# Moving the output projection of the third segment behind the opening of the feed-forward buffers

## The chip, the cores and the metric

The kernel runs on one core of a Trainium2 chip. The core has a matrix engine (TensorE, "PE" in the profile, with its weight loads as "PEld"), a vector engine (VectorE, "DVE"), a scalar engine (ScalarE, "ACT"), a general engine (GpSimd, "POOL") and a queue engine that issues the transfers (SyncE, "SP"). Each engine takes its instructions strictly in the order in which they were written for it, and waits for the others by semaphores. The metric is the device time of one execution in microseconds (us), as the median of several runs.

## The reference

One layer over x of 2048 rows and 512 columns, with 32 heads of 16 columns, four segments of 512 rows, and a feed-forward width of 1792:

```python
mod = (_silu(c) @ w_mod).reshape(c.shape[0], 6, 1, -1)
sa, ca, ga, sb, cb, gb = (mod[:, 0], mod[:, 1], mod[:, 2], mod[:, 3], mod[:, 4], mod[:, 5])
h = _layernorm(x, axis=-1) * (1 + ca) + sa
x = x + ga * _A_ref(h, A_wq, A_wk, A_wv, A_wo, A_beta)
h = _layernorm(x, axis=-1) * (1 + cb) + sb
x = x + gb * _B_ref(h, B_w1, B_b1, B_w2, B_b2)
```

`_A_ref` is softmax attention inside each segment of 512 rows (with the mask of the code), mixed by a gate with a linear memory that is summed over the segments before. Its result is multiplied by `wo`: that is the output projection of this text. `_B_ref` is `relu(x @ w1 + b1)**2 @ w2 + b2`.

## The kernel before

**Numbers.** Matrix products are done three times on operands split into a rounded high part and a low part (high*high, high*low, low*high). ACT writes the high part with a cast; DVE or POOL writes the low part as the difference. Most work around the change is of this kind: one cast and one subtraction for each operand tile.

**Stages.** The first stage (to about 431 us) goes over sixteen units `u`: segment `s = u // 4`, eight heads at a time. For each unit it makes queries and keys (`qk`), values (`vproj`), row maxima (`a_quad`), then scores, exponentials, masks and value products (`b_quad`: scores on TensorE at L1144, exponentials on ACT at L1161, masks on POOL at L1148, value products on TensorE at L1203, transposes back at L1238, normalisation on DVE at L1252 to L1255, the sum with the memory's part at L1261), and the memory (`mem`). In the last segment the heads' results stay on the chip in `X1L`; those of the first three go to DRAM (`o_dram`).

The output projection works on sixteen tiles of 128 rows (`wo_tile(g, pr)`, L1313), four for each segment. A tile loads its heads' results and its rows of x (L1321, L1322), turns them (L1332), splits them into a high part on ACT (L1340) and a low part on DVE (L1342), multiplies by `wo` (held in `WVO`), adds x, takes the statistics for the second normalisation (`ln_stats`, L631, L632) and stores the sum as x1 (L1377). Tiles of segments 0 to 2 (`last` false) multiply in two half-height shapes of 64 rows and 256 columns that TensorE runs in pairs (L1358): 48 products a tile. Tiles of segment 3 (`last` true) use 12 full products of 128 rows and 512 columns (`wo_mm`, L1306 to L1308).

The second normalisation for a segment is `ln2(s, pr)` (L1381): a reciprocal root on POOL (L636, L637), then for each tile the application on DVE (L640), transposes, and an affine step on ACT and DVE (L1398, L1400) into `h2raw`. `h2_ops(s, at)` (L1419) makes the seven operands B11, B12 and so on of a fast product of two-by-two blocks with seven multiplications: differences on POOL (L1438), high parts on ACT (L1446), low parts on DVE (L1448).

The second stage is the feed-forward part. `ffn1(s, p)` multiplies a segment's operands with pair `p` of W1 columns (seven pairs for each segment, seven products each at L1652, sums on DVE at L1664 and L1668, the squared ReLU at L1682 to L1686). `ffn2(s, i, p)` multiplies the result with W2 (L1737) and sums over `p`. W1 is prepared during attention, lies in DRAM and is fetched anew for each segment in halves of 1 MB and 0.75 MB (`fetch_w1`, L1581) into three buffers. W2's seven pairs are multiplied with the gate and combined on POOL (`make_w2`, L817, L818), and split on ACT and DVE (L834, L835); pair 0 is built in `w2a`, pairs 2 to 5 in their buffers, and pairs 1 and 6 go through DRAM (`VIA`).

**Memory.** `open_late` (L1273) takes over the place of the projection weights once the last queries, keys and values are made; it brings `h2raw`, `w2a`, five row tiles `T5`, and a pool `wop` with two tiles `oT` for the projection's split inputs. `open_ffn` (L1535) closes the pool of the attention stage (`ph1`) and `wop`, and opens the feed-forward buffers in their place (W2 tiles, the third W1 buffer, `Tx`, the work space `W2s`). A new tile waits only for the users of the old tiles under it. The tiles of segment 3 split their inputs into the third W1 buffer (two tiles, `FF["ot"]`) and into `FF["ao"]`.

**Order.** The program is a list of nodes, made in the order of the code; each has an engine, what it comes after, and what buffers it takes (`get`) and gives back (`put`). `ORDER` gives for each engine the whole order of its nodes, as node numbers. `N_LATE` and `N_FFN` are nodes without work that run `open_late` and `open_ffn`; `N_FFN` comes after every node made before it except a few. TensorE's row of work near the end of attention is the projection tiles of segments 0 to 2 one after the other, product by product, between the scores and value products of units 13 to 15; behind the last value product come the first feed-forward products of segment 0 and the four tiles of segment 3 between them.

```python
    N_FFN = op("NIL", 0.0, open_ffn, -20.0, after=[n for n in PL.nodes if n.seq not in free_of])
    ...
    for t in range(4):
        wo_tile(4 * NS - 4 + t, z - 2 + 0.3 * t)
```

Of the kernel before, what the change touches and what calls it, by code (L numbers as in the profile page):

```python
# [8 lines left out]
F32 = mybir.dt.float32  # L9
# [8 lines left out]
P = 128  # L18
# [61 lines left out]
1878 496 1879-1880 1971 2128 2333 1974 2334 1978 2140 2335 2122 2336 1986 1882 2338-2339 1981 2340 2131 2341 2143 2259  # L80
1990-1992 1994 2457 1997 2458 2264 2459-2460 2267 2001 2152 2462 2004 2463 2238 2246 2464-2465 2249 2009 2013 2270
2159 2014-2015 2273 498 2166 2162 2276 2252 2169 2243 2362 2178 2599 2174 1968 2179 2280 2182 2255 2180 2404 2185 2189
2017 2616 2192 2602-2605 2367 2370 2607 2197 2608-2610 2373 2201-2203 2633 2283 2376 2619-2620 2290 2621-2622 2205
2286 2624-2627 2383 2636-2638 2379 2639 2391 2298 2293 2641-2644 2397 2667 2650 2302-2304 2306 2653 2313 2654-2656
2309 2670-2671 2658 2672-2673 2388 2659-2661 2394 2675 2735 2316 2676-2678 2321 2738 2486 2739-2741 2494 2684 2400
2743-2746 2407 2491 2752 2325-2327 2414 2687 2422 2497 2688-2690 2755 2500 2756 2692-2694 2417 2695 2757-2758 2507
2521 2410 2760-2763 2430 2329 2433 2849 2701 2426-2427 2503 2437 2440 2518 2428 2845 2769 2837 2841 2449-2450 2445
2704-2707 2512 2531 2709-2711 2538 2772-2773 2712 2774 2515 2775 2534 2451 2777 2541 2778 2524 2779 2546 2780 2453
2718 2786 2550-2552 2721 2554 2722-2723 2561 2724 2789 2564 2790 2726-2727 2791-2792 2728 2557 2729 2794 2569 2795
2528 2796-2797 2573-2575 2996 2577 2997 2999 2874 2896 2907 2998 3001-3002 2885 2877-2879 2910-2911 3017-3018 2912  # L90
3019 2913 2899 3020 2880 3000 2900 2888 2901 2889 3348 2902 3338 2890-2891 3022-3023 3353 3038 3021 3041 3039-3040
# [329 lines left out]
def block_kernel(ctx, tc, x, wq, wk, wv, wo, beta, w1, b1, w2, b2, c, wmod, out):  # L421
# [851 lines left out]
    def open_late():  # L1273
# [562 lines left out]
```

## Time and profile before

| what | us |
|---|---|
| median of 3 runs | 751.4 (751.25, 751.4, 754.45) |
| the profiled execution, its own time | 753.9 |
| its span, first to last instruction | 751.8 |
| TensorE busy in the span | 728.3 |
| DVE, ACT, POOL busy | 631.6, 487.3, 490.3 |
| twelve half-height projection tiles (L1358), TensorE busy | 42.5 |
| mean granted TensorE clock | 0.996 |

The profile is of one execution. The time of an execution holds 2.1 us around the span. "Busy" of TensorE counts overlapping products once; a product's record is longer than its step in a row of equal products, so the length of a row is read from the start of its first product to the start of what follows. "Idle before <-releaser" names the work whose end let the engine go on. The rows themselves stand in the prediction.

### The profile page before, as it was taken

The numbers are of one execution on the slowest core, as the hardware profiler recorded it, in microseconds if no ns is written. First come the engines' busy times: TensorE is split into PE (matmuls) and PEld (weight loads), VectorE is DVE, ScalarE is ACT, GpSimd is POOL, SyncE is SP. The second block draws the span as 40 slices with busy tenths as digits, with TensorE's granted clock in tenths as the row PEclk, the third lists the DMA queues.
The fourth block names the chain that finished last, engine by engine and source line by source line (L and its number), as shares of the span: only waits on it lengthen the run. The fifth ranks groups of instructions, "written<-read, shape, count | busy, mean of one in ns | idle before, by whom it ended". The sixth has DMA issues, their size and how long they took to land.

```text
span 751.8 us, 20671 instructions
## 1 busy us (share of the span) xinstructions
PE 728.3 (97%) x7549; PEld 616.1 (82%) x7549; DVE 631.6 (84%) x1684; ACT 487.3 (65%) x1074; POOL 490.3 (65%) x669
## 2 busy tenths in 40 slices
PE   8999999999999999999999989999999999999996
PEld 7776777666777677776787778999999999999996
DVE  5588888898898989889998989788798888867785
ACT  3669877999879986888668836574335442543342
POOL 5776857789858785664775467857555755555662
PEclk9999999999999999999999999999999999999999
DMA  9887864545643454557893188997776677657710
GB/s 312 249 221 238 246 170 125 161 115 163 199 140 101 111 168 100 142 154 248 259 324 117 49 285 287 327 326 268 251 275 235 224 229 240 231 199 241 277 43 29
DMA packets 84608, 151.84 MB, mean 202 GB/s; under 512 B 10134, under 2 KB 32666, under 8 KB 84508
## 3 DMA queue, kind: packets, MB, share of 16 engines
q1 hardware_dynamic: 84356, 150.40, 63.5%
q8 instruction: 60, 0.98, 0.5%
q14 instruction: 40, 0.33, 0.1%
q10 hardware_dynamic: 152, 0.13, 0.1%
HBM read 94.14 MB, written 29.36 MB: 164 GB/s over the span
## 4 chain that ended last, share of the span: by engine, by line
PE 72%; DVE 10%; DMA 9%; ACT 3%; issue 3%; SPq 2%; POOL 1%; DVEq 0%; ACTq 0%; POOLq 0%
PE bm L1737 16%; PE bh L1652 14%; PE bpv L1203 8%; PE bqk L867 7%; PE bv L937 5%; PE ba L975 5%; PE bpb L1144 5%; DMA ST<-w1d 4%; PE bwop L1358 4%; DVE ba L980 2%; DMA ST<-sg 2%; SPq L916 2%; PE bwarm L570 2%; DMA xt<-in_A_x 1%; ACT pt L1161 1%
## 5 line engine op out<-in xcount | busy, mean ns | idle before, releaser
L980 DVE CUSTOM_DVE_ANT_0 ba<-ba,msk 128x384 f32<-128x384 f32 (+2 forms) x384 | 193.0, 531 | 28.0 <-PE ba L975 21.2
L1161 ACT ACTIVATE pt<-bpb 128x512 f32<-128x512 f32 x320 | 174.2, 617 | 11.7 <-PE bpb L1144 10.3
L1148 POOL TENSOR_SCALAR_AFFINE_SELECT pt<-pt 128x512 f32<-128x512 f32 x128 | 79.5, 641 | 66.8 <-ACT pt L1161 43.5
L867 PE MATMUL bqk<-HT,WQK 64*128 64x512 f32 x720 | 104.6, 397 | 0.3 <-ACT HT L843 0.3
L1737 PE MATMUL bm<-w,ST 128*128 128x256 f32 x660 | 94.0, 283 | 1.0 <-DVE ST L1722 0.5
L1737 PEld LDWEIGHTS bm<-w,ST 128*128 128x128 f32 x660 | 85.2, 191 | 1.5 <-DVE ST L1722 0.7
L1203 PE MATMUL bpv<-pt,VT 128*32 128x512 f32 (+3 forms) x1024 | 82.3, 441 | 0.3 <-ACT lnf L657 0.2
L1144 PE MATMUL bpb<-ST 64*128 64x256 f32 (+2 forms) x512 | 80.7, 345 | 1.8 <-DMA ST<-mt 1.1
L1652 PE MATMUL bh<-ST 128*128 128x256 f32 x564 | 79.8, 283 | 2.1 <-DVE ST L1448 2.0
L867 PEld LDWEIGHTS bqk<-HT,WQK 64*128 64x128 f32 x720 | 70.4, 185 | 9.6 <-ACT VT L943 0.8
L975 PE MATMUL ba<-ST 63*128 63x256 f32 (+2 forms) x512 | 76.1, 340 | 1.8 <-DMA ST<-sg 0.9
L1652 PEld LDWEIGHTS bh<-ST 128*128 128x128 f32 x564 | 72.5, 190 | 3.0 <-DVE ST L1448 2.2
L975 PEld LDWEIGHTS ba<-ST 63*128 63x128 f32 x512 | 51.1, 185 | 20.2 <-DVE mx L980 2.5
L1144 PEld LDWEIGHTS bpb<-ST 64*128 64x128 f32 x512 | 52.2, 185 | 18.5 <-issue 3.9
L1203 PEld LDWEIGHTS bpv<-pt,VT 128*32 128x32 f32 x1024 | 27.6, 109 | 33.8 <-issue 25.0
L980 DVE DVE_READ_ACCUMULATOR2_ANT mx<- 128x1 f32 x384 | 54.3, 141 | 0.1
L937 PE MATMUL bv<-WVO,HT 64*128 64x512 f32 x384 | 54.1, 395 | 0.0
L909 POOL TENSOR_SCALAR e<-e 128x512 f32<-128x512 f32 x24 | 35.7, 1489 | 15.4 <-ACT e L905 15.0
L1358 PE MATMUL bwop<-WVO,oT 64*128 64x256 f32 x576 | 42.5, 280 | 0.2 <-DVE am L1078 0.2
L1358 PEld LDWEIGHTS bwop<-WVO,oT 64*128 64x128 f32 x576 | 39.4, 185 | 1.9 <-DVE am L1078 0.5
L937 PEld LDWEIGHTS bv<-WVO,HT 64*128 64x128 f32 x384 | 37.0, 185 | 4.7
L1008 ACT COPY ac<-ba 128x512 f32<-128x512 f32 x64 | 36.0, 600 | 7.1 <-PE ba L975 6.9
(299 smaller groups left out, 1724.4 us busy)
## 6 DMA issues: line engine op xcount, KB each, us to landing
ST<-sg SPq DMA_DIRECT2D x192, 128.0 KB
ST<-w1d SPq DMA_DIRECT2D x20, 1024.0 KB
ST<-w1d SPq DMA_DIRECT2D x18, 768.0 KB
w1d<-X1L SPq DMA_DIRECT2D x21, 512.0 KB
w<-w1d SPq DMA_DIRECT2D x8, 1024.0 KB
w<-w1d SPq DMA_DIRECT2D x10, 768.0 KB
xt<-in_A_x SPq DMA_DIRECT2D x16, 256.0 KB
wm<-in_w_mod SPq DMA_DIRECT2D x16, 256.0 KB
```

Source lines behind the costliest of these rows:

```text
L867: nc.tensor.matmul(bank(banks[w]), W3(w, k, x, cols.start, cols.stop)[r], HT[r, y, k], start=first and i == 0, stop=last and i == 2)
L937: nc.tensor.matmul(bank(banks[t]), HT[r, x, k, (t2 + t) * P:(t2 + t + 1) * P], WVO[r, k, y], start=first and i == 0, stop=last and i == 2)
L975: nc.tensor.matmul(dst[:, c0:c0 + n], ST[b:b + 63, 0, sl, qt * P:(qt + 1) * P], ST[b:b + 63, 1, sl, :n], start=True, stop=True)
L980: nc.vector.tensor_tensor_reduce(i, i, msk[:, 512 - n:], scale=1.0, scalar=-3e38, op0=ALU.add, op1=ALU.max, accum_out=o)
L1008: cp = [act(512, lambda j=j: nc.scalar.copy(buf("ac", ac)[:, j], bank(keys[j])), pr[0] + 0.01 + 0.001 * j, after=[first], put=[keys[j]]) f ...
L1144: nc.tensor.matmul(dst, ST[b:b + 64, 1, sl, kb * P:(kb + 1) * P], ST[b:b + 64, 0, sl, q0:512], start=True, stop=True)
L1148: nc.gpsimd.affine_select(out=ap, in_=ap, pattern=[[0, ap.shape[1]], [1, P]], compare_op=ALU.is_ge, fill=0.0, base=0, channel_multiplier=-1)
L1161: ns = [op("ACT", 0.49, lambda j=j: nc.scalar.activation(buf("PPP"[n], pt)[:, i + j], bank(keys[j]), AF.Exp, scale=0.25), pr[slot] + 0.01 ...
L1203: nc.tensor.matmul(bank(o)[32 * hq:32 * hq + 32, q0:q0 + src.shape[1]], v[:, a:a + 32], src, start=start, stop=stop, tile_position=(0, 32 ...
L1358: nc.tensor.matmul(bank(bs_[c])[:, :256], TL[ot][r, x, k * P:(k + 1) * P], WVO[r, k, y, 256 * c:256 * c + 256], start=turn == i == q == 0, ...
L1652: nc.tensor.matmul(pb(i), A[:, x, kk], B[:, y, kk], start=kk == j == 0, stop=kk == 1 and j == 2)
L1737: nc.tensor.matmul(q if wide else q[:, c * HALF:(c + 1) * HALF], TL[ao][a >= 3][:, x, a_ * P:(a_ + 1) * P], LT["w2z"][:, b:15:14 - b] if w ...
```

## The change

It does six things.

1. `wo_tile` distinguishes `last = s >= 2` (segments 2 and 3) from `end = s == 3`. The tiles of segment 2 are no longer made before `N_FFN` but behind the tiles of segment 3, and use the 12 full products of the `last` branch. Their loads of heads' results and x, and their stores, move with them.
2. All sixteen tiles split their inputs into two tiles `LT["oT"]` that lie in `w1c`, a tile that `open_late` opens and that later is the third W1 buffer. The pool `wop` and `FF["ot"]` go. The third W1 buffer is given free (`("w1h",)`) when all eight last tiles have multiplied.
3. The tiles of segment 3 no longer wait for `N_FFN`; their loads of x come after `N_LATE`. The four tiles `Tx` are held back from the pool of row tiles until `N_FFN` (`("txh",)`).
4. Six low parts go from DVE to POOL: three of W2 pair 0 (`p == W2R`) and three of segment 0's operands (B11, T1, B21).
5. `ln2` of segments 1 to 3 no longer waits for all four x loads of segment 3, and some planned times change.
6. `ORDER` is written anew for all five engines, from about the third unit of segment 2 to the end. In it POOL's subtractions of W2 pair 0 stand among the masks of units 13 and 14, that of T1 among the masks of unit 15, and those of B11 and B21 directly behind the last mask. TensorE's order begins the feed-forward part with S2\*T2, the last transposes, A22\*T4 and A11\*B11, then tiles 14, 13, 15 and 12 (segment 3) and 8, 9, 11 and 10 (segment 2) between the products of pairs 0 to 3. Which W2 pairs are built in their buffers and which go through DRAM stays as it was (pairs 0 and 2 to 5 in place, 1 and 6 through DRAM).

```diff
-            l = op("DVE", (b - a) * HALF / 960 + 0.07, lambda a=a, b=b, o=o: nc.vector.tensor_tensor(
+            gp = p == W2R
+            l = op("POOL" if gp else "DVE", ((b - a) * HALF / 500 + 0.2) if gp else (b - a) * HALF / 960 + 0.07, lambda a=a, b=b, o=o: (nc.gpsimd if gp else nc.vector).tensor_tensor(
...
-        LT["s"] = ExitStack()
-        LT["op"] = LT["s"].enter_context(tc.tile_pool(name="wop", bufs=1, side="right", reuse_waits="tile"))
+        LT["w1c"] = x1p.tile([P, 2, 4, 2, P], F32R, name="w1c")
+        LT["oT"] = [LT["w1c"].rearrange("p h a k n -> p (h a k n)")[:, i * 2 * L:(i + 1) * 2 * L].rearrange("p (h n) -> p h n", h=2) for i in (0, 1)]
...
-        last = s == NS - 1
+        last, end = s >= WL, s == NS - 1
...
-        ld = sp(load, pr - 0.2, 1 << (18 if last else 19), 1 if last else 2, after=heads + [N_FFN if last else N_LATE],
-                get=[("xr", xk)] if last else [("xr", o), ("xr", xk)])
+        ld = sp(load, pr - 0.2, 1 << (18 if end else 19), 1 if end else 2, after=[N_LATE] if end else heads + [N_LATE],
+                get=[("xr", xk)] if end else [("xr", o), ("xr", xk)])
...
-                       after=[n] if k else [h, l, *WON], get=() if k else [("#D", b2)], put=[ot if g % 2 else ("w1h",)] if k == KD - 1 else ())
+                       after=[n] if k else [h, l, *WON], get=() if k else [("#D", b2)], put=[ot, ("w1h",)] if k == KD - 1 else ())
...
-        r = op("POOL", 1.33, lambda: ln_rstd(st_all[:, 4 * s:4 * s + 4]), pr[0] - 0.1, after=[X1N[4 * s + t] for t in range(4)] + (XWN if s else []))
+        r = op("POOL", 1.33, lambda: ln_rstd(st_all[:, 4 * s:4 * s + 4]), pr[0] - 0.1, after=[X1N[4 * s + t] for t in range(4)])
...
+            gp = s == 0 and j in (0, 3, 6)
+            l = op("POOL" if gp else "DVE", 1.24 if gp else 0.6, lambda j=j, name=name: (nc.gpsimd if gp else nc.vector).tensor_tensor(
...
+    PL.held["txh",] = [("T", i) for i in range(5, 9)]
+    for i in range(9):
...
-    for s in range(NS - 1):
+    WL = 2
+    for s in range(WL):
         for t in range(4):
             wo_tile(4 * s + t, e + K_P[s] + 0.3 * t)
...
-        LT["s"].close()
...
-                    for i in (0, 1)] + [sb2.tile([P, 2, 4, 2, P], F32R, name="w1")]
+                    for i in (0, 1)] + [LT["w1c"]]
...
+    for t in range(4):
+        wo_tile(4 * NS - 8 + t, us(3 + 3.5 * t))
...
-        make_w2(p, 2 + 7 * i, (("W2s", 4 * (i % 2)), ("W2s", 2)), ("W2s", 6), [N_FFN, *(WOL if p == W2C else ()), *W2Q.get(p - 2 if i > 1 else None, ())], [n_gb2],
+        make_w2(p, 6 + 7 * i, (("W2s", 4 * (i % 2)), ("W2s", 2)), ("W2s", 6), [N_FFN, *(WOL if p == W2C else ()), *W2Q.get(p - 2 if i > 1 else None, ())], [n_gb2],
...
-            ln2(s, [us(T0 - 34 + 5 * t) for t in range(4)])
+            ln2(s, [us(T0 - 26 + 3.5 * t) for t in range(4)])
```

More of the change, by code (lines that the diff above doesn't have):

```diff
@@ L199 @@
+4257 4321 4261-4262 4265 4331 4240 4333 4343 4345 4242 4354-4355 4357 4371 4373 4356 4360 4358-4359 4362 4361 4383
+4363 4385 4259 4395 4258 4397 4260 4407 4409 4419 4421 4431 4433 4443 4445 4455 4457 4454 4460-4461 4456 4463
+4458-4459 4462
 """,
@@ L1314, in wo_tile @@
         s = g // 4
-        last = s == NS - 1
+        last, end = s >= WL, s == NS - 1
         o, xk, b, b2, ot = ("ot", g), ("xw", g), ("wot", g), ("wop", g), ("oT", g)
-        pool = "ao" if last else "oT"
         def load():
-            if not last:
+            if not end:
                 nc.sync.dma_start(buf("xr", o), o_dram[g * P:(g + 1) * P, :])
@@ L1330, in tr @@
             for k in range(KD):
-                src = X1L[:, g % 4] if last else TL[o]
+                src = X1L[:, g % 4] if end else TL[o]
                 nc.tensor.transpose(bank(b)[:, k * P:(k + 1) * P], src[:, k * P:(k + 1) * P], ident)
-        n = pe("F", 0.355, tr, pr, after=heads + [N_FFN] if last else [ld], get=[("#D", b)] if last and g % 2 == 0 else [("#D", b), (pool, ot)], put=[("on3", g % 4)] if last else [o])
+        n = pe("F", 0.355, tr, pr, after=heads if end else [ld], get=[("#D", b), ("oT", ot)], put=[("on3", g % 4)] if end else [o])
         def hi():
-            if last:
-                TL[ot] = FF["ao"][PL.slot[ot]][1] if g % 2 else FF["ot"][g % 4 // 2]
-            else:
-                TL[ot] = LT["op"].tile([P, 2, D], F32R, name="oT", tag=f"oT{PL.slot[ot]}")
+            TL[ot] = LT["oT"][PL.slot[ot]]
             nc.scalar.copy(TL[ot][:, 0], bank(b))
@@ L1447, in halves @@
                     after=[*([node[name]] if name in node else RAW[s]), *wait], put=put)
-            l = op("DVE", 0.6, lambda j=j, name=name: nc.vector.tensor_tensor(operand(j)[:, 1], blk[name](), operand(j)[:, 0].bitcast(F32),
-                                                                            op=ALU.subtract), at[1 + j] + 0.05, after=[h], put=put, lock=True)
+            gp = s == 0 and j in (0, 3, 6)
+            l = op("POOL" if gp else "DVE", 1.24 if gp else 0.6, lambda j=j, name=name: (nc.gpsimd if gp else nc.vector).tensor_tensor(
+                operand(j)[:, 1], blk[name](), operand(j)[:, 0].bitcast(F32), op=ALU.subtract), at[1 + j] + 0.05, after=[h], put=put, lock=True)
             OPN[s][name] = [h, l]
@@ L1469, in block_kernel @@
     PL.held["w2t",] = [("T", i) for i in range(5)]
-    for i in range(5):
+    PL.held["txh",] = [("T", i) for i in range(5, 9)]
+    for i in range(9):
         PL.pools["T"].remove(i)
@@ L1561, in block_kernel @@
     free_of = {n.seq for n in h2_ops(0, [us(-7 + 0.7 * j) for j in range(8)]) + W2S}
-    N_FFN = op("NIL", 0.0, open_ffn, -20.0, after=[n for n in PL.nodes if n.seq not in free_of])
+    N_FFN = op("NIL", 0.0, open_ffn, -20.0, after=[n for n in PL.nodes if n.seq not in free_of], put=[("txh",)])
     HOME["xr"] = "T"
```

195 lines of the change are left out of this document (96 added, 99 removed), and 13 rows, old and new, of the table ORDER.

## The prediction

> **What bounds the kernel now.** I read the page first, then the stretches ("windows"), then the timeline of TensorE with its waits. Page, engine shares and chain:
>
> ```profile
> PE 728.3 (97%) x7549; PEld 616.1 (82%) x7549; DVE 631.6 (84%) x1684; ACT 487.3 (65%) x1074; POOL 490.3 (65%) x669
> PE 72%; DVE 10%; DMA 9%; ACT 3%; issue 3%; SPq 2%; POOL 1%; DVEq 0%; ACTq 0%; POOLq 0%
> ```
>
> TensorE is busy for 728.3 of 751.8 us. The most that any reordering can win is the remaining 23.5 us. By stretch (columns: PE, PEld, DVE, ACT, POOL busy us; granted clock; DMA share; GB/s):
>
> ```profile
> 0.00:100.00 100.00, 94.97 (x1010) 74.82 (x1011) 74.53 (x218) 71.59 (x163) 72.57 (x95) 1.00 0.84 253
> 350.00:431.00 81.00, 80.77 (x1143) 65.08 (x1135) 74.53 (x218) 60.52 (x133) 50.29 (x65) 1.00 0.59 195
> 431.00:451.00 20.00, 16.48 (x119) 14.34 (x120) 17.29 (x34) 7.47 (x14) 11.44 (x10) 1.00 0.87 285
> 451.00:485.00 34.00, 32.27 (x243) 30.33 (x242) 29.40 (x58) 18.40 (x37) 26.42 (x33) 1.00 0.87 298
> 485.00:732.00 247.00, 243.17 (x2013) 240.80 (x2012) 202.39 (x405) 110.28 (x217) 147.15 (x233) 1.00 0.70 237
> 732.00:751.80 19.80, 13.26 (x111) 13.05 (x109) 11.48 (x19) 5.31 (x10) 6.46 (x9) 0.94 0.08 28
> 344.00:348.00 4.00, 4.00 (x57) 1.69 (x53) 3.43 (x9) 2.69 (x6) 1.44 (x2) 0.66 0.44 118
> ```
>
> Of the 23.5 us, 5.0 lie in the first 100 and 6.5 in the last 20, where this change does nothing or little. From 350 to 431 us the last attention units run with the twelve output-projection tiles of segments 0 to 2 between them, and TensorE has 0.2 us idle. It loses 3.52 us at the border (431 to 451), 1.73 us from 451 to 485, and 3.8 us in the whole feed-forward stretch behind. DVE is at 74.5 of 81 us in the attention stretch, so it is next. The last row shows a granted clock of 0.66 over 4 us; the third that is missing is worth some 1.4 us. The waits at the border and just after (start, duration, operation, idle before and what ended it):
>
> ```profile
> 435.36 1.20 PE L1332 MATMUL bwot<-ident,X1L 128*128 128x128 f32 x9 [0.93 <-DVE X1L L1261]
> 440.07 0.86 PE L1652 MATMUL bh<-ST 128*128 128x256 f32 x5 [1.96 <-DVE ST L1448]
> 445.50 1.66 PE L1652 MATMUL bh<-H2o,ST 128*128 128x256 f32 x12 [0.63 <-DMA ST<-w1d]
> 460.25 0.97 PE L1652 MATMUL bh<-H2o,ST 128*128 128x256 f32 x6 [0.52 <-DMA ST<-w1d]
> 474.50 0.95 PE L1652 MATMUL bh<-ST,w 128*128 128x256 f32 x6 [0.58 <-DMA w<-w1d]
> 483.19 0.94 PE L1652 MATMUL bh<-H2o,ST 128*128 128x256 f32 x6 [0.63 <-DMA ST<-w1d]
> ```
>
> These six, 5.25 us, are what this change can address.
>
> **The change part by part.**
>
> (1) Four tiles (segment 2) leave the attention stretch and come back behind the border, in another shape: 48 half-height products of 256 columns in pairs before, 12 full products of 512 columns after.
>
> ```profile
> 417.16 1.10 PE L1332 MATMUL bwot<-ident,ot 128*128 128x128 f32 x8
> 418.18 2.36 PE L1203 MATMUL bpv<-pt,VT 128*32 128x512 f32 x32
> ...
> 423.17 2.29 PE L1358 MATMUL bwop<-WVO,oT 64*128 64x256 f32 x36
> 425.28 0.40 PE L1144 MATMUL bpb<-ST 64*128 64x512 f32 x2
> ...
> 441.44 0.40 PE L1307 MATMUL bwop<-WVO,w 128*128 128x512 f32 x1
> 444.47 0.40 PE L1308 MATMUL bwop<-WVO,ST 128*128 128x512 f32 x1
> ```
>
> Old shape: 36 from 423.17 to 425.28, 0.0586 us each, so 48 take 2.81 us. New shape: the second to the fifteenth of a row start 441.44 and 444.47, 13 steps of 0.233 us, so 12 take 2.80 us. The transposes are the same on both sides (two tiles 417.16 to 418.18 with the change of shape, about 0.4 us each). Removed: 4 x 3.2 = 12.8 us; added: 4 x 3.2 us. The work of TensorE is **conserved, 0.0 us**. Attention should end some 12 us earlier, near 419 us, and the feed-forward part grows by as much.
>
> (2) Changes of shape. The written TensorE order changes between full, half-height and quarter-width products 142 times before and 147 times after; all five more lie in the attention stretch, where fewer projection products stand between score and value products.
>
> ```profile
> 427.73 0.95 PE L1358 MATMUL bwop<-WVO,oT 64*128 64x256 f32 x11
> 428.61 2.36 PE L1203 MATMUL bpv<-pt,VT 128*32 128x512 f32 x32
> 430.90 0.97 PE L1652 MATMUL bh<-H2o,ST 128*128 128x256 f32 x6
> ```
>
> Eleven products from 427.73 at 0.0586 us end their stream at 428.37; the next shape starts at 428.61: 0.24 us. I take 0.2 x 5 = **+1.0 us** (0 if all fall into waits, 1.2 at most). The Trainium skill, TensorEngine Tiling (Array Packing), Key Properties, says that a change of tiling mode drains TensorE; it gives no price. By that rule each of the five costs, which the gap above agrees with; without it the sum would be 1.0 us lower.
>
> (3) The border. The other engines in the old tail:
>
> ```profile
> 425.58 1.58 ACT L1161 ACTIVATE pt<-bpb 128x512 f32<-128x512 f32 x3
> 431.04 0.59 ACT L1227 COPY oraw<-bpv 128x512 f32<-128x512 f32 x1 [1.52 <-PE bpv L1203]
> 425.46 0.68 DVE L1448 TENSOR_TENSOR ST<-tt,ST 128x512 fp32r<-128x512 f32 x1
> 438.87 1.15 DVE L1448 TENSOR_TENSOR ST<-h2raw,ST 128x512 fp32r<-128x512 f32 x1
> 437.43 3.74 POOL L818 TENSOR_TENSOR W2s<-W2s 128x512 f32<-128x512 f32 x2 [7.16 <-PE bh L1652]
> 421.29 1.30 POOL L1438 TENSOR_TENSOR tt<-tt,h2raw 128x512 f32<-128x512 f32 x1 [1.59 <-DVE H2o L1448]
> ```
>
> The 1.96 us wait goes: that low part (B21, the 1.15 us row) ran beside POOL's W2 work and stood in DVE's queue behind a W2 part (L835); the new order has both on POOL and asks for B21 seventeen groups after the last value product. What is late next? Let E be the end of the last value product. ACT starts its copy about 0.25 us after E (the next product starts at 430.90 after a change of shape, so E is near 430.8; the copy starts at 431.04), and in the new ACT order two casts stand behind it, B22 and then B11, at about 0.5 us pitch: B11's high part is there at E+1.9. Its low part is now on POOL, 1.3 us instead of 0.68: with two handoffs of about 0.25 it reaches TensorE at E+3.7. Before product A11*B11 TensorE has only S2*T2 (0.71), the last transposes (0.5) and A22*T4 (0.71) with their shape changes, 2.5 us: it waits 1.2 us. The X1L sum (L1261) then comes at about the time that this product ends. Next, the first segment-3 tile needs its high part (ACT behind two other casts) and its low part on DVE: another 0.8 us. The last exponentials (0.52 us each by the first row, ten behind the last scores) and the two masks on POOL behind them hold the last value products for 0.1 to 0.9 us; I count 0.4. Sum 2.4 against 3.52: **-1.1 us** (bounds: none of it saved, and all 3.52 saved).
>
> (4) The first W1 loads. With eight tiles instead of four between the products of the first pairs, TensorE asks for W1 more slowly; but the third W1 buffer is the new home of all projection inputs, and it comes free only after the last of the eight. I counted in the order, from the last use of a buffer to the next need: 8.8, 7.1, 8.5, 11.6, 7.8 and 7.0 us of TensorE work. How long a load takes with the queue full:
>
> ```profile
> 452.35 0.53 SPq L1581 DMA_DIRECT2D ST<-w1d  x1
> ```
>
> The load issued at 452.35 is the one that the product at 460.25 waited for: about 7.9 us with others before it (298 GB/s in that stretch; 1 MB alone would be 3.5 us at that rate). So the spans of 7.0 to 8.8 us are about enough, no more. SP's queue gets eight more loads and four stores here, the loads in order behind the first W2 load: if that waits for memory, the W1 load of the second pair waits behind it. In return the four projection stores that held SP for 13.29 us (below) are fewer. As to bytes: 3 MB, 10 us at 298 GB/s, come with 12.8 us more of TensorE work. I take half of the 1.73 us of waits from 451 to 485 as saved: **-0.9 us** (bounds -1.7 and, if loads come late in the same measure, +1.7).
>
> (5) DVE and ACT.
>
> ```profile
> L1342 DVE TENSOR_TENSOR oT<-bwot,oT 128x512 fp32r<-128x512 f32 x12 | 8.1, 685 | 0.7 <-ACT oT L1340 0.6
> 426.06 0.76 DVE L1370 TENSOR_TENSOR xw<-bwop,xw 128x256 f32<-128x256 f32 x2
> 427.33 0.69 DVE L631 BATCH_NORM_STATS2 bs<-xw 128x6 f32<-128x512 f32 x1
> 428.05 0.18 DVE L632 BATCH_NORM_AGGREGATE st_all<-bs 128x2 f32<-128x6 f32 x1
> ```
>
> Per tile DVE has 0.69 + 0.76 + 0.69 + 0.18 = 2.3 us, 9.3 us in four (ACT, at 60.5 of 81 us, loses one cast a tile). They return behind the border, where DVE has room (202 of 247 us). The subtractions that go to POOL take some 2 us more off DVE before E. That leaves DVE about (74.5 - 9.3 - 2) of 69 us, 92% as before: hidden by TensorE's own work as before, **0**. With that cover gone (4) and (3) would carry it: each us that DVE is late at the border is a us of the end.
>
> (6) The end.
>
> ```profile
> 744.39 0.52 PE L1737 MATMUL bm<-WVO,ST 128*128 128x256 f32 x3
> 744.75 0.51 PE L1737 MATMUL bm<-w,ao 128*128 128x256 f32 x3
> 748.27 0.41 DVE L1771 TENSOR_TENSOR Tx<-Tx,bm 128x256 f32<-128x256 f32 x1
> ```
>
> These two short groups, 0.36 us apart, are the last of TensorE, and ten DVE sums in a row end the kernel 3 us behind them. In the new order the first of the two stands before the groups that the sums start with, so the sums start 0.36 us later against TensorE's end: **+0.35 us**, on the path.
>
> (7) Everything else in the feed-forward order is reshuffled; its 3.8 us of idle I take as unchanged (0, bounds -1.9 and +1.9).
>
> Sum: 0.0 + 1.0 - 1.1 - 0.9 + 0.35 = **-0.65 us** against the profiled execution, which took 753.9 us by its own time (span 751.8 and 2.1 around it). That execution lies 2.5 us above the median of the three runs (751.4); I take the difference off the median: **750.7 us**. A measurement of this kernel can tell about 0.5% (3.8 us) from no change.
>
> **The rivals.**
>
> *Faster: the idle time really goes.* For it: eight independent tiles are cover that the old order lacked at just the place where the W1 loads were late; the SP queue waited long for projection stores (below) and is freed earlier. Then the 1.73 us goes, half of the 3.8, the border falls to 1.5 us (-2.0), and the low clock at 344 us does not return (-1.4): 1.35 - 1.7 - 1.9 - 2.0 - 1.4 = -5.7, **745.7 us**. Against it: at the place of the low clock the new order is nearly the old one, and DVE is as full.
>
> ```profile
> 418.08 13.29 SPq L1377 DMA_DIRECT2D x_dram<-xw  x4
> ```
>
> *Slower: POOL's queue holds the masks.*
>
> ```profile
> L1148 POOL TENSOR_SCALAR_AFFINE_SELECT pt<-pt 128x512 f32<-128x512 f32 x28 | 17.7, 646 | 23.1 <-ACT pt L1161 16.9 <-PE bpv L1203 2.1 <-issue 2.1
> ```
>
> POOL gets six subtractions, five of 512 columns at 1.3 us and one of 768, by its length 1.9 us: 8.4 us; before the last value products alone it rises from 50.3 of 81 us (62%) to about 56 of 69 (81%). Four stand in POOL's queue directly among the masks that the value products need, and the pair at 437.43 took 3.74 us, not 2.6, beside a DVE subtraction (438.87). If half of the 8.4 us reaches TensorE, the price is 4.2 us with nothing won: **755.6 us**. It decides once a subtraction stands ahead of a mask whose exponentials are done by more than it lasts. Against it: between 350 and 431 us POOL waited 16.9 us for exponentials before its masks (the row); a queue that waits so much has room. By the Trainium skill, SBUF — State Buffer, Who interferes with whom, a DVE operation with two SBUF inputs and a POOL operation that reads SBUF block each other in full; the 1.15 us row agrees. By that rule the shift makes each such block twice as long, not shorter, which would add up to 6 x 0.6 = 3.6 us.
>
> *The change doesn't do what it says.* The buffers of the feed-forward part lie where attention's own tiles lay, so opening them earlier in the order may start no load earlier: then (4) is 0, and the time is 751.6 us, no change either.
>
> **How the numbers follow.** Forecast with the third rival (both within 0.5%): 0.50. Faster by over 0.5% (below 747.6): 0.31. Slower by over 0.5% (above 755.2): 0.19. The likeliest case itself runs from 748.0 to 754.0; the range reaches into both rivals, with the bounds of (3), (4) and (7) added: 745.6 to 755.8.
>
> **What would show it.** Right: the last value product ends near 419 us; the six waits fall to about 3 us together, one of about 1 us before the product with H2o (L1652) waiting for POOL; no waits for masks above 1 us. Wrong: TensorE idle before value products (L1203) with POOL as the releaser (slower rival), or feed-forward idle from 470 us on under 2 us (faster rival). Three things make the prediction wrong: a clock below 1.0 at the border, a DMA wait of several us behind SP's new loads, or a total idle that moves by more than 4 us in the reshuffled part.

## The result, and the profile after

| what | before | after |
|---|---|---|
| median, 9 runs each on one chip (us) | 754.45 (751.25 to 757.16) | 748.59 (744.37 to 750.32) |
| ratio, 95% interval | 1 | 0.9916 (0.9888 to 0.9945) |
| profiled execution, its own time | 753.9 | 746.45 |
| its span | 751.8 | 744.7 |
| TensorE busy | 728.3 | 724.5 |

The change makes the kernel faster by 0.84%, 6.3 us of 754.45 (4.1 to 8.4 by the interval). The forecast was 0.65 us less, too little to be told from no change, so that its sign came out says little. The gain is that of the rival "the idle time really goes" (-5.7). That the median of 748.59 lies in the stated range, and even in the 748.0 to 754.0 of the likeliest case, is in part luck: the range was counted from 751.4, the median of three runs of the kernel before, and nine runs of it have 754.45. The line of engine shares on the page of the kernel after:

```profile
PE 724.5 (97%) x7405; PEld 612.3 (82%) x7405; DVE 623.7 (84%) x1674; ACT 485.7 (65%) x1070; POOL 495.5 (67%) x675
```

The share of TensorE is 97%, as before. To see where the 7.1 us of span went, cut both executions at 322 us (until about there TensorE's order is the same), at the first feed-forward product, and at the end of TensorE's last product. Stretches of the kernel before (span, busy us of PE, PEld, DVE, ACT, POOL; granted clock; DMA share; GB/s):

```profile
322.00:430.90 108.90, 107.93 (x1426) 82.29 (x1422) 98.86 (x293) 84.14 (x185) 63.80 (x82) 0.98 0.60 192
430.90:745.20 314.30, 305.22 (x2484) 298.62 (x2480) 257.44 (x508) 141.46 (x277) 191.48 (x282) 1.00 0.70 237
```

The same of the kernel after:

```profile
322.00:419.40 97.40, 93.65 (x1215) 67.83 (x1212) 88.40 (x273) 79.12 (x174) 69.71 (x86) 1.00 0.62 196
419.40:738.40 319.00, 316.07 (x2548) 308.01 (x2544) 258.98 (x519) 144.54 (x284) 191.22 (x284) 1.00 0.71 239
```

Attention ends 11.5 us earlier (108.9 to 97.4). The feed-forward part grows by 4.7 (314.3 to 319.0), though TensorE is busy 10.85 us longer in it: its idle time there falls from 9.08 to 2.93 us. In attention the idle time grows, from 0.97 to 3.75. TensorE's waits in the kernel after (start, duration, operation, idle before and what ended it), and the last value product with the first feed-forward product behind it:

```profile
345.98 0.22 PE L1041 MATMUL bat<-ident,mx 64*16 64x64 f32 x1 [1.37 <-DVE tm L1121]
347.75 0.56 PE L976 MATMUL ba<-ST 63*128 63x256 f32 x4 [1.26 <-DVE on L1256]
352.57 1.17 PE L1069 MATMUL bmr<-MB,phi 64*128 64x68 f32 x16 [1.07 <-ACT ac L1009]
...
416.65 2.79 PE L1204 MATMUL bpv<-pt,VT 128*32 128x256 f32 x40
419.38 0.97 PE L1652 MATMUL bh<-H2o,ST 128*128 128x256 f32 x6
...
422.55 0.86 PE L1652 MATMUL bh<-H2o,ST 128*128 128x256 f32 x5 [0.53 <-POOL H2o L1446]
...
456.18 0.50 PE L1309 MATMUL bwop<-WVO,w1c 128*128 128x512 f32 x1 [0.24 <-DVE w1c L1339]
...
492.80 1.67 PE L1652 MATMUL bh<-ST 128*128 128x256 f32 x12 [1.14 <-DMA ST<-w1d]
```

The six waits of before, 5.25 us from 435 to 483, have become one of 0.53 us and one of 0.24 before 485, and one of 1.14 at 492.80. The first has the place and the releaser that the prediction named for A11\*B11 (the low part of B11 on POOL), and half the length. The three in front are new.

### The profile page after: what moved, and what is told of

Same layout as the page of the kernel before. It is cut to its first block, busy times and chain, and to the rows that moved or that the text cites. A ratio compares the mean times of both kernels' runs of the same rounds, so it can differ in the third digit from the quotient of the medians.

```text
span 744.7 us, 20355 instructions
## 1 busy us (share of the span) xinstructions
PE 724.5 (97%) x7405; PEld 612.3 (82%) x7405; DVE 623.7 (84%) x1674; ACT 485.7 (65%) x1070; POOL 495.5 (67%) x675
## 5 line engine op out<-in xcount | busy, mean ns | idle before, releaser
L981 DVE CUSTOM_DVE_ANT_0 ba<-ba,msk 128x384 f32<-128x384 f32 (+2 forms) x384 | 192.9, 531 | 26.9 <-PE ba L976 19.8
L1652 PE MATMUL bh<-ST 128*128 128x256 f32 x600 | 84.4, 283 | 1.1 <-DMA ST<-w1d 1.1
L1652 PEld LDWEIGHTS bh<-ST 128*128 128x128 f32 x600 | 77.1, 190 | 2.0 <-ACT H2o L1443 1.3
L779 POOL TENSOR_TENSOR X1L<-X1L 128x512 fp32r<-128x512 f32 (+1 forms) x28 | 32.2, 1149 | 12.4 <-ACT X1L L778 12.0
L1020 DVE TENSOR_REDUCE mx<-ac 128x4 f32<-128x1024 f32 x32 | 38.9, 1215 | 0.3 <-POOL ac L1017 0.2
```

What stands on the lines that cost most here:

```text
L981: nc.vector.tensor_tensor_reduce(i, i, msk[:, 512 - n:], scale=1.0, scalar=-3e38, op0=ALU.add, op1=ALU.max, accum_out=o)
L1020: reds.append(op("DVE", 1.13, lambda: nc.vector.tensor_reduce(buf("mx", mx).rearrange("p (a t) -> p a t", t=4)[:, :, 1], acv(), axis=AX.X, ...
L1652: nc.tensor.matmul(pb(i), A[:, x, kk], B[:, y, kk], start=kk == j == 0, stop=kk == 1 and j == 2)
```

## The experiments

Names that begin with b_ are variants of the kernel before, those with a_ of the changed kernel; what each leaves out or moves is told below. Each ratio is to the kernel before on the same chip. For all fourteen profiles, three places can be compared: a mark that every kernel has near 140 us (the value products that wait for the logarithm, 140.94 in the kernel before and 140.91 after), the first feed-forward product (E), and the end of TensorE's last product (745.26 before, 738.45 after). The mark takes out what the first 140 us differ by from execution to execution, up to 3.2 us. The places come from one profiled execution of each kernel, the ratios from 6 to 12 runs.

| kernel | E | mark to E | E to TensorE's end | ratio to before, 95% interval |
|---|---|---|---|---|
| before | 430.90 | 290.0 | 314.4 | 1 |
| b_pool6 | 434.83 | 293.9 | 316.8 | 1.0017 (0.9986 to 1.0047) |
| b_less | 430.76 | 290.5 | 315.0 | 0.9999 (0.9970 to 1.0027) |
| b_dve | 431.31 | 289.1 | 312.7 | 0.9996 (0.9971 to 1.0020) |
| b_both | 427.73 | 287.6 | 313.8 | 0.9971 (0.9948 to 0.9994) |
| b_none | 432.89 | 293.2 | 312.2 | 0.9979 (0.9951 to 1.0006) |
| after | 419.38 | 278.5 | 319.1 | 0.9916 (0.9888 to 0.9945) |
| a_dve6 | 419.90 | 279.4 | 319.8 | 0.9922 (0.9896 to 0.9948) |
| a_less | 420.14 | 280.0 | 319.3 | 0.9930 (0.9900 to 0.9960) |
| a_both | 422.15 | 280.5 | 318.4 | 0.9911 (0.9877 to 0.9946) |
| a_less_w1half | 421.69 | 280.3 | 318.6 | 0.9916 (0.9887 to 0.9945) |
| a_none | 421.51 | 280.3 | 319.9 | 0.9896 (0.9848 to 0.9944) |
| a_oldtail | 421.57 | 280.1 | 320.7 | 0.9955 (0.9929 to 0.9981) |
| a_fix | 418.52 | 279.5 | 321.6 | 0.9947 (0.9922 to 0.9973) |

The table is the main finding. Two groups appear: every kernel with the old order takes 288 to 294 us from the mark to E, and 312 to 317 behind it; every kernel with the new order takes 278 to 281 and 318 to 322. What work of the moved tiles is left out hardly matters in either group.

**The six low parts.** The changed kernel with them back on DVE (the diff), and the kernel before with them on POOL (the same two lines the other way round); in `ORDER` their six numbers move between the lists of the two engines:

```diff
-            gp = p == W2R
+            gp = False
...
-            gp = s == 0 and j in (0, 3, 6)
+            gp = False
```

> The changed kernel with its six low parts (three of W2 pair 0, and B11, T1, B21 of segment 0) back on DVE, each as late in DVE's order as its reader allows; everything else as changed. Theory A (cover: the eight independent projection tiles stand between the first feed-forward products, so that operands and W1 halves come in time, wherever the low parts are made): the time stays within 1.5 us of the changed kernel, 0.990 to 0.994 of the kernel before, and TensorE's idle time behind the last value product stays under 4.5 us (2.9 in the changed kernel). Rival B (POOL: the border is better because six low parts left DVE): 3 to 5 us slower than the changed kernel, 0.996 to 0.999, with a wait of 1.5 to 2 us for a low part of DVE back at the border.

> The kernel before with the same six low parts on POOL, placed behind the masks that are due; nothing else of the change. Theory A (cover): no gain, 0.997 to 1.004 of the kernel before; the wait of 1.96 us for B21's low part may go, but the other waits from the border to 485 us stay (over 3 us together). Rival B (POOL): 2 to 3.5 us faster, 0.995 to 0.997, with the border's 3.52 us of idle under 1.5.

Theory A held both times. On DVE the changed kernel has 0.9922 against 0.9916, and the border's waits stay about 1 us:

```profile
422.01 0.86 PE L1652 MATMUL bh<-ST 128*128 128x256 f32 x5 [0.18 <-DVE ST L1446]
423.45 0.85 PE L1652 MATMUL bh<-H2o,ST 128*128 128x256 f32 x5 [0.47 <-DVE H2o L1446]
425.02 0.77 PE L1332 MATMUL bwot<-ident,X1L 128*128 128x128 f32 x5 [0.39 <-DVE X1L L1262]
```

So in the changed kernel the wait of 1.96 us for B21 goes without POOL too, since B21 is asked for later there. In the kernel before, the same shift alone gains nothing that can be measured. Its profiled execution is 757.8 us long against 751.8: attention took 3.9 us more from the mark, and a W1 load was late by 4 us:

```profile
450.52 2.90 PE L1654 MATMUL bh<-H2o,ST 128*128 128x256 f32 x12 [4.11 <-DMA ST<-w1d]
```

So the 1.96 us wait did go in it, and others took its place (7.3 us of waits from E to 490 us).

**Less TensorE work, in the new place and in the old.** In a_less a tile of segment 2 makes 3 of its 12 products, in b_less 12 of its 48:

```diff
-                n = pe("F", 0.699, lambda k=k: wo_mm(bank(b2), TL[ot], k), ...
+                n = pe("F", 0.699, lambda k=k: wo_mm(bank(b2), TL[ot], k) if s > 2 else wo_one(bank(b2), TL[ot]) if k == 0 else None, ...
```
```diff
             def mm(turn, k, i):
+                if s == 2 and i != (KD - 1 if turn else 0):
+                    return
```

> The changed kernel with 9 of the 12 products of each tile of segment 2 left out (the tile's transposes, splits, sum, loads and stores stay): 36 products of 0.233 us, 8.4 us of TensorE work between the first feed-forward products. Theory A (cover: these products hide the W1 loads): W1 waits come back, 1.5 to 3.5 us of them between the last value product and 480 us, and the time falls by 5 to 7 us only (0.982 to 0.985 of the kernel before). Rival (the loads are in time because they are issued earlier, not because of the cover): it falls by the full 8.4 us (0.980).

> The kernel before with the same share left out: 36 of the 48 half-height products of each tile of segment 2, 144 products of 0.0586 us, 8.4 us of TensorE work in the attention stretch. If TensorE bounds that stretch (0.2 us idle in 81), the last value product comes 7 to 8.4 us earlier and the time falls by as much (0.989 to 0.991). If DVE is as near to the bound as its 74.5 of 81 us say, TensorE begins to wait for DVE there: 3 to 6 us (0.992 to 0.996), and what the move won in attention is less than the 12.8 us of the work.

Both fell short of every number that stood there: 0.9930 (the changed kernel has 0.9916) and 0.9999. In the new place all 8.4 us are given back. Waits of a_less:

```profile
455.12 0.48 PE L1312 MATMUL bwop<-WVO,w1c 128*128 128x512 f32 x1 [3.08 <-DVE uuT L1669]
456.81 0.79 PE L1314 MATMUL bwop<-WVO,w1c 128*128 128x512 f32 x1 [0.98 <-DVE w1c L1344]
466.09 2.58 PE L1657 MATMUL bh<-ST 128*128 128x256 f32 x12 [2.11 <-DMA ST<-w1d]
```

These are 6.17 us, and the granted clock from 439 to 475 us is 0.91 (the row stands further below). In the old place the work leaves a stretch that the profile had shown as full, and E stays where it was. The row of b_less for it:

```profile
322.00:430.80 108.80, 104.47 (x1274) 74.75 (x1270) 99.43 (x290) 83.09 (x184) 64.62 (x82) 0.98 0.59 191
```

144 products of 0.0586 us are gone, 8.4 us, but "busy" fell only from 107.93 to 104.47, 3.5 us, and 3.4 us appear as idle time. The other 5 us still count as busy. The likely reason, which was not tried by itself, is the length of the records: a half-height product that stands alone has a record of 0.28 us (the products at 353.69 and 355.61 in the kernel before) against its step of 0.0586, so short waits between products vanish under the records.

**DVE's part, alone and together with TensorE's.** b_dve leaves out most of DVE's sum and statistics for the four tiles; b_both and a_both have both cuts.

```diff
-            n = [dve(256, lambda c=c: nc.vector.tensor_tensor(TL[xk][:, 256 * c:256 * c + 256], ...
+            n = [dve(256, lambda c=c, n_=8 if s == 2 else 256: nc.vector.tensor_tensor(TL[xk][:, 256 * c:256 * c + n_], ...
...
-        X1N[g] = op("DVE", 0.8, lambda: ln_stats(TL[xk], st_all[:, g]), ...
+        X1N[g] = op("DVE", 0.8, lambda: nc.vector.memset(st_all[:, g], 1.0) if s == 2 else ln_stats(TL[xk], st_all[:, g]), ...
```

> The kernel before with part of DVE's work on the four tiles of segment 2 left out: the two statistics instructions of a tile become one small write, and the sums with x shrink from 256 to 8 columns; by the rows 0.87 and some 0.6 us a tile, 5.5 to 6 us of DVE work in four, at the place in the attention stretch where the same tiles' TensorE work was cut without effect. TensorE's work is whole. If DVE alone sets the pace of that stretch, the last value product (430.8 in the kernel before) comes 4 to 5.5 us earlier and the time falls by as much (0.993 to 0.995). If both engines are at their limit there, or the pace is set by ACT or by the loop between them, it falls by under 1.5 us (0.998 to 1.000).

> The kernel before with both cuts: 8.4 us of TensorE work (36 of 48 products a tile) and 5.5 to 6 us of DVE work of the tiles of segment 2. If DVE and TensorE are both at their limit in the attention stretch, so that neither cut alone does anything: the last value product 4.5 to 6 us earlier, time 0.991 to 0.994. If DVE alone sets the pace: the same as with the cut on DVE alone, within 1 us. If neither does (ACT's exponentials): under 1.5 us.

> The changed kernel with the same two cuts on the tiles of segment 2, which now stand between the first feed-forward products (TensorE's cut alone brought 0 there: waits of 3.1 and 1.0 us for DVE and of 2.1 us for a W1 load came in its place). If DVE, 92% busy from 439 to 475 us, is the limit: 3 to 6 us faster than the changed kernel (0.983 to 0.988 of the kernel before). If the loads are the limit (309 GB/s in that stretch): within 1.5 us of the changed kernel, with the W1 waits longer than 2.1 us.

DVE alone brings nothing (0.9996). Both cuts, some 14 us of work on two engines, bring 2.2 us (0.9971), and 2.4 us from the mark to E: well under the 4.5 to 6 us named for two engines at their limit, and above the 1.5 us named for neither. In the new place both bring nothing beyond the changed kernel (0.9911); its waits from 455 to 468 us are 2.65 and 0.98 us for DVE and 2.25 us for a W1 load, nearly those of a_less. So DVE, 92% busy as it is, isn't the bound by itself either.

**The loads.** The changed kernel with TensorE's cut and half of segment 0's W1 bytes:

```diff
-        n = sp(lambda: nc.sync.dma_start(FF_w1(key)[:, :, :n_].bitcast(F32), w1_dram[p][:, :, a:a + n_]), ...
+        n = sp(lambda: nc.sync.dma_start(FF_w1(key)[:, :1 if s == 0 else 2, :n_].bitcast(F32), w1_dram[p][:, :1 if s == 0 else 2, a:a + n_]), ...
```

> The changed kernel with TensorE's cut (36 products of segment 2's tiles) and with only the high parts of W1 fetched for segment 0, which halves the 12.25 MB of these fetches; the products read what lies in the low places. If the loads are the limit where TensorE's cut alone brought nothing: 4 to 8 us faster than the changed kernel (0.980 to 0.986 of the kernel before), and the W1 wait near 466 us is gone. If DVE is the limit: under 2.5 us faster, with the waits for DVE near 455 us as they were (3.1 and 1.0 us).

The W1 wait at 466 is gone and the time is the same (0.9916). The waits for DVE stay and others come:

```profile
457.43 0.76 PE L1312 MATMUL bwop<-WVO,w1c 128*128 128x512 f32 x1 [3.83 <-DVE uuT L1669]
459.12 0.79 PE L1314 MATMUL bwop<-WVO,w1c 128*128 128x512 f32 x1 [0.50 <-DVE w1c L1344]
476.98 0.66 PE L644 MATMUL blnq<-ident,X1L 128*128 128x128 f32 x4 [1.56 <-DVE X1L L640]
```

There DVE has 34.56 us of 36 busy (439 to 475), without the tiles' sums being cut. So neither the cut on DVE (a_both) nor that on the loads brings the time down: it seems that loads and DVE's results stand close behind each other, and between them the tiles' products are free. A kernel relieved of both was not made, so this stays an argument.

**No engine work of the four tiles at all.**

```diff
-            for k in range(KD):
+            for k in range(KD if s != 2 else 0):
...
-        h = act(512, hi, pr + 0.01, after=[n], put=[b])
-        l = dve(512, lambda: nc.vector.tensor_tensor(TL[ot][:, 1], ...
+        h = act(512, hi if s != 2 else lambda: None, pr + 0.01, after=[n], put=[b])
+        l = dve(512, lambda: None if s == 2 else nc.vector.tensor_tensor(TL[ot][:, 1], ...
```

(and the products, the sums and the statistics likewise)

> The kernel before without any engine work of segment 2's four projection tiles (transposes, casts, differences, products and sums left out, the statistics one small write; loads and stores stay). Cutting 8.4 us of TensorE work there brought nothing, cutting DVE too brought about 2 us. If the attention stretch is held by TensorE, DVE and ACT in turn, so that only the whole of a tile's work counts: the last value product comes 10 to 12.5 us earlier than 430.8 and the time falls by 8 to 12 us (0.984 to 0.989). If the pace there is set by something that the tiles have no part in: under 5 us (above 0.993), and the changed kernel's 11.6 us must come from its new order.

> The changed kernel without any engine work of the same four tiles. If they stand in time in which TensorE would otherwise wait for operands and loads: within 2 us of the changed kernel (0.988 to 0.992 of the kernel before), with 8 us or more of waits behind the last value product. If they cost there what the two profiles differ by behind the last value product: 4 to 5 us faster than the changed kernel. If TensorE's work is conserved, as the prediction had it: 11 to 12.8 us faster (0.975).

In the new place the four tiles cost nothing that can be measured (0.9896 without them, 0.9916 with them, each inside the other's interval). The 11 to 12.8 us of conserved work (0.975) are excluded. The 4 to 5 us of the second number are not excluded by a_none's wide interval (0.9848 to 0.9944) alone; against them stand its length from E (319.9 us, 319.1 in the changed kernel) and the three kernels with part of the tiles' work left out (0.9911 to 0.9930). The stretch from 439 to 475 us of the changed kernel, of a_less and of a_none:

```profile
439.00:475.00 36.00, 35.76 (x244) 32.39 (x242) 33.04 (x63) 20.27 (x38) 21.02 (x27) 1.00 0.89 314
```
```profile
439.00:475.00 36.00, 29.83 (x201) 27.60 (x200) 33.65 (x64) 18.97 (x35) 19.64 (x26) 0.91 0.89 309
```
```profile
439.00:475.00 36.00, 26.97 (x171) 24.99 (x171) 28.10 (x55) 16.86 (x32) 19.17 (x28) 0.86 0.91 318
```

TensorE is idle for 0.24, 6.17 and 9.03 us in it. With 14% of a busy 26.97 us lost to the clock, an estimate of 3.8 us, a_none loses 12.8 us here: as much as the four tiles' TensorE work, which the prediction had put at 4 x 3.2. The waits that fill it:

```profile
447.77 1.65 PE L1652 MATMUL bh<-H2o,ST 128*128 128x256 f32 x12 [1.36 <-DMA ST<-w1d]
456.37 2.55 PE L1652 MATMUL bh<-ST 128*128 128x256 f32 x12 [4.04 <-DVE uuT L1668]
460.19 2.90 PE L1652 MATMUL bh<-H2o,ST 128*128 128x256 f32 x12 [1.27 <-DVE h2raw L1397]
467.28 2.93 PE L1652 MATMUL bh<-ST 128*128 128x256 f32 x12 [2.36 <-DMA ST<-w1d]
```

In the old place they cost nearly nothing either: 0.9979, and E is no earlier. The row of b_none:

```profile
322.00:432.90 110.90, 103.73 (x1209) 72.79 (x1205) 94.48 (x279) 79.86 (x175) 65.00 (x82) 0.95 0.61 197
```

The granted clock is 0.95 in it against 0.98 before, which on 103.73 busy us is some 3 us more lost; without that E would stand about where it does in the kernel before, still no earlier. So the tiles' work going away is not enough: with the old order it can go, and attention lasts as long. How much the order does shows where most of the gain arises. Six groups of 32 value products into the stretch (the sixth starts at 387.67 us before, at 385.73 after), the changed kernel is 2 us ahead; the other 9.5 us come in the last four groups. These last groups in the kernel before, in b_none and in the kernel after:

```profile
390.10:430.90 40.80, 40.80 (x587) 32.84 (x585) 37.19 (x107) 34.41 (x75) 18.66 (x26) 1.00 0.29 100
```
```profile
392.50:432.90 40.40, 38.16 (x433) 25.54 (x433) 31.38 (x94) 32.63 (x70) 19.07 (x26) 0.96 0.36 126
```
```profile
388.10:419.40 31.30, 31.30 (x435) 22.77 (x431) 27.78 (x87) 28.86 (x65) 21.61 (x27) 1.00 0.51 168
```

With nearly the same products (433 and 435), the old order takes 40.4 us and the new one 31.3. Taking 154 products out of the old order wins 0.4 there. The new order is thus needed for the gain. Whether it would win as much with the tiles still in attention isn't shown: in the changed kernel the trace has no gap of TensorE left in these 31.3 us. And "the new order" means here all that b_none keeps as before: it still has the four tiles' loads, stores and buffers in the old place, and no run moves these alone.

**What in the order.** At the end of attention in b_none ACT stands out. Some of its instructions there (start, duration, operation):

```profile
421.39 0.62 ACT L1446 CAST H2o<-tt 128x512 fp32r<-128x512 f32 x1
...
426.10 3.03 ACT L1161 ACTIVATE pt<-bpb 128x512 f32<-128x512 f32 x6
428.97 0.66 ACT L1446 CAST ST<-h2raw 128x512 fp32r<-128x512 f32 x1
429.48 0.88 ACT L834 CAST w2a<-T 128x768 fp32r<-128x768 f32 x1
430.21 1.14 ACT L1161 ACTIVATE pt<-bpb 128x512 f32<-128x512 f32 x2
```

Casts of the feed-forward part stand in ACT's queue in front of the last exponentials, and ACT has few gaps. The kernel before is alike: of the 16 us from 414 to 430 ACT is busy for 15.22.

```profile
414.00:430.00 16.00, 16.00 (x242) 12.91 (x238) 14.49 (x41) 15.22 (x32) 7.25 (x10) 1.00 0.10 35
```

There six casts of operands and two of W2 stand among the last exponentials; in the last 16 us of the kernel after it is two of operands and none of W2, and the other operand casts come behind the last exponentials (417.81 to 420.52):

```profile
411.49 0.62 ACT L1443 CAST H2o<-tt 128x512 fp32r<-128x512 f32 x1
412.01 4.25 ACT L1162 ACTIVATE pt<-bpb 128x512 f32<-128x512 f32 x8
416.84 1.09 ACT L1162 ACTIVATE pt<-bpb 128x512 f32<-128x512 f32 x2 [0.58 <-PE bpb L1145]
417.81 0.62 ACT L1443 CAST ST<-tt 128x512 fp32r<-128x512 f32 x1
```

Six casts of 0.5 us would be 3 us of the 11.5, if ACT set the pace. But ACT is nearly as full in the kernel after:

```profile
403.40:419.40 16.00, 16.00 (x249) 10.94 (x241) 13.57 (x40) 14.74 (x32) 11.75 (x13) 1.00 0.57 183
```

This is read from the traces, no run moved these casts alone, and a full ACT is no better a proof of a bound than a full TensorE was. Which part of the order wins the time stays open.

**The order of the rest, and one swap.** a_oldtail has the order of the kernel before on all engines from about 505 us on. a_fix changes five entries of DVE's order (2594 and 2582 are multiplications of wo by the gate at L1298, 1969 the difference at L1121, 2018 and 2019 the normalisations at L1253 to L1256):

```diff
-2594 1969 2582 2018-2019
+1969 2018-2019 2594 2582
```

> The changed kernel with the order of the kernel before on all five engines from about 505 us on; the tiles, the border and the first pairs as changed. If the part of the gain behind 485 us (idle 3.8 us before, 1.9 after) comes from the newly written order: 1 to 2.5 us slower than the changed kernel, with waits of about 1 us back behind 505 us. If it comes from what lies ahead (loads in time, queues without backlog): within 0.7 us.

> The changed kernel with one swap in DVE's order: the first multiplication of wo by the gate, which waits 1.7 us for its load near 343 us, goes behind the memory's masked difference and the two normalisations of unit 11 that stand behind it in DVE's queue and that TensorE waits for (1.37 and 1.26 us). If these waits delay the rest of attention: the last value product comes 1.5 to 3 us earlier than in the changed kernel and the time falls by as much, 0.986 to 0.990 of the kernel before. If attention is held by other engines behind it anyway: within 0.7 us of the changed kernel though the two waits are gone.

a_oldtail has 0.9955, 2.9 us more than the changed kernel by the middle of the intervals, which overlap. From E to TensorE's end it takes 320.7 us against 319.1, and waits return:

```profile
526.08 0.97 PE L1652 MATMUL bh<-H2o,ST 128*128 128x256 f32 x6 [0.48 <-DMA ST<-w1d]
...
661.46 0.94 PE L1652 MATMUL bh<-H2o,ST 128*128 128x256 f32 x6 [1.45 <-DMA ST<-w1d]
```

This agrees with some 1.6 us of the gain lying in how the rest of the feed-forward part is ordered, but one execution doesn't show it: the other kernels with the rest in the new order take 318.4 to 321.6.

a_fix was an attempt to beat both kernels. The changed kernel's two waits at 346 and 348 us come from one DVE instruction that waits for a load at the head of its queue:

```profile
345.12 0.69 DVE L1298 TENSOR_TENSOR wo<-wo,gab 128x512 f32<-128x512 f32 x1 [1.74 <-DMA wo<-in_A_wo]
```

Behind the swap the two waits are gone, waits of 1.06, 0.37 and 0.92 us stand in their place, and E is no earlier from the mark (279.5 against 278.5). Behind E, 2.07 us of waits for DVE appear where the changed kernel has 0.24:

```profile
344.92 0.66 PE L1332 MATMUL bwot<-ident,ot 128*128 128x128 f32 x4 [1.06 <-ACT mt L1043]
...
351.66 1.65 PE L1355 MATMUL bwop<-WVO,w1c 64*128 64x256 f32 x11 [0.92 <-DVE den L1076]
...
455.67 0.47 PE L1307 MATMUL bwop<-WVO,w1c 128*128 128x512 f32 x1 [1.08 <-DVE uuT L1664]
457.36 0.80 PE L1309 MATMUL bwop<-WVO,w1c 128*128 128x512 f32 x1 [0.99 <-DVE w1c L1339]
```

The ratio is 0.9947: nothing won, and neither of the two numbers of the expectation met. No kernel of the study beats the changed one by more than the measurement tells.

## Why the prediction was right in its sign and wrong in its size

- **(1) TensorE's work is conserved; attention ends near 419.** The place was right to half a microsecond (first feed-forward product 419.38). The reason was wrong as it stands. The step took "80.77 of 81 us busy" to mean that each microsecond of TensorE work taken out shortens the stretch by one; b_less took out 8.4 us and b_none all of it, and neither moved E forward. It came out because the new order went with it, which the step gave no part; that is luck in the mechanism. And it took the work to cost its own length again behind the border; a_none shows that there it costs nothing measurable. The feed-forward part grew by 4.7 us, not by 12.8, and it has that length without the tiles too (319.9 us).
- **(2) Five more changes of shape, +1.0.** Neither shown nor refuted. Busy time from 322 us to E fell by 14.3, of which 1.4 is the low clock at 344 us that didn't return, and rose by 10.85 behind E. But b_less shows that busy time moves by 3.5 us for 8.4 us of products, so a term of 1.0 us can't be read from it.
- **(3) The border, -1.1.** Mis-sized: in the 20 us behind E idle time went from 3.52 to 0.53 us, -3.0. The wait for B11 on POOL came, at 0.53 for 1.2; those for the first tile of segment 3 and for the masks, 1.2 us together, didn't.
- **(4) The first W1 loads, -0.9.** Mis-sized: of the 1.73 us 0.24 is left, a wait for DVE, and one wait of 1.14 us for a load came at 492.80, behind the stretch: -1.5. The reason given, more independent work while the loads run, is what a_less and a_none support: take that work out and the loads are waited for again (2.11 us; 1.36 and 2.36 us). The loads behind the first two are also issued earlier: the third to the sixth at 6.4, 13.2, 20.0 and 23.3 us behind E, where the kernel before has 6.8, 19.8, 21.5 and 24.9. No run tells the two apart. The count of "spans of 7.0 to 8.8 us against a load of 7.9" was too pessimistic.
- **(5) DVE as full as before, 0.** Right as far as it went: cutting its part alone changes nothing (b_dve, 0.9996). The step looked at ACT as 60.5 of 81 us, an average that hides the 16 us from 414 on, where ACT had 15.22; whether that mattered isn't shown.
- **(6) The end, +0.35.** From TensorE's end to the end of the span 6.5 us before and 6.25 after: -0.3.
- **(7) The rest of the feed-forward order, 0.** It won about 1.7 us of idle time (3.83 from 485 us on before, 2.16 from 475 us on after); a_oldtail gives some of it back, so the new order may have a part in it.

The step that failed is therefore in (1): the reading of a full TensorE as the bound, and with it the full price of the work in its new place. From E to TensorE's end the forecast adds up to +10.8 us (12.8 - 1.1 - 0.9), and the stretch grew by 4.7. Of these 6.1 us, 4.15 lie in (3), (4) and (7), -2.0 together where idle time fell by 6.15, and 1.95 in busy time that rose by 10.85 and not by 12.8. Inside attention 2.8 us of new waits appeared. The prediction had named a total idle that moves by more than 4 us in the reshuffled part as a sign of being wrong: counted from E on it came (6.15 us), in the part behind 475 us alone it didn't (1.7). The faster rival's sign, under 2 us of idle from 470 us on, was missed narrowly (2.16). The slower rival, POOL's queue in front of the masks, didn't show: no value product of the changed kernel waits for POOL near the border. That the change doesn't do what it says, so that the W1 waits stay, is refuted by (4).

## What to carry to other kernels

A busy share near 100% is no proof of a bound: leave part of that engine's work out and see whether the end moves, before a moved piece of work is priced at its own length. In this program, whose queues are ordered by hand, work that was dropped without a new order was given back as waits. So the price of moved work was what the waits around the new place left over, and the gain at the old place was what the new order made of it. Look at the last microseconds of a stretch engine by engine, too: an average over 80 us can hide an engine that is full over the last 16. That is where to try a cut, not yet a cause.

## What the runs showed of the hardware

Gaps in TensorE's work can cost more than their length. In a_none TensorE was busy for 1.12 of the 4 us from 344 on, and then ran 4 us at half clock (busy us and granted clock as above):

```profile
344.00:348.00 4.00, 1.12 (x14) 0.39 (x6) 2.71 (x6) 2.67 (x8) 1.67 (x2) 0.98 0.94 314
348.00:352.00 4.00, 3.73 (x22) 2.20 (x26) 3.90 (x12) 2.82 (x8) 0.63 (x1) 0.50 0.95 306
352.00:356.00 4.00, 4.00 (x51) 2.63 (x44) 3.47 (x10) 2.67 (x7) 0.00 (x0) 0.67 0.86 266
```

Those 8 us lose 3.2 us, as much as the 3.15 us of waits in front of them (1.88 and 1.27). Seven of the eight profiles with the new order have such a dip between 348 and 356 us, behind the waits there. The changed kernel itself doesn't, with 1.37 of 4 us busy and a clock of 1.00 behind. Its row, and that of a_dve6 for the same place behind waits of 1.32 and 1.27 us:

```profile
344.00:348.00 4.00, 1.37 (x18) 0.64 (x10) 2.77 (x8) 3.19 (x9) 2.19 (x2) 1.00 0.94 311
348.00:352.00 4.00, 3.50 (x40) 1.78 (x38) 3.93 (x11) 2.82 (x8) 0.63 (x1) 1.00 0.96 324
```
```profile
348.00:352.00 4.00, 4.00 (x34) 2.04 (x34) 3.96 (x10) 2.91 (x7) 0.40 (x1) 0.57 1.02 335
```

The length of the waits alone doesn't decide: 2.63 us in two pieces passed in the changed kernel, while 2.59 in a_dve6 and 2.50 in a_less were followed by 4 us at a granted clock of 0.57 and 0.50.

The Trainium skill, TensorE: Matmul & The Clock Gate, What's actually happening, says that TensorE falls to half clock after an idle window of about 3.4 us and comes back after a busy window of the same length. The half clock and its some 4 us agree with the rows; but it fell here behind two waits of 3.15 us together with 0.51 us of work between them, and behind shorter ones too. So work that is taken away can come back twice, as idle time and as a low clock: the 12.8 us of a_none from 439 to 475 are, by the estimate above, 9.0 of the one and 3.8 of the other.
